# Gated linear attention and a squared-ReLU network on one core: another order of the opening, and attention stretches, weight parts and splits at other places between the products

## The chip, the cores and the metric

The kernel runs on one core of a Trainium2 chip. The core has TensorE (products, PE in the profile, with its weight loads as PEld), VectorE (DVE), ScalarE (ACT), GpSimd (POOL) and SyncE (SP, which issues all transfers here). The metric is the time of one execution on the device, in microseconds; less is better. The profile comes from one execution of its own.

## The reference

Per batch and head, a 48 x 48 state decays by alpha and takes in the outer product of k and v; y is q times the state. The rows of y (all heads side by side, 384 wide) are the input of a network with a squared ReLU.

```python
# B, H, S, D = 4, 8, 768, 48
for t in range(S):
    state = alpha[:, :, t, :, None] * state + einsum('bhd,bhde->...', k[:, :, t], v[:, :, t])
    y[:, :, t] = einsum('bhd,bhde->bhe', q[:, :, t], state)
...
x = y.transpose(0, 2, 1, 3).reshape(3072, 384)
h = np.maximum(x @ w_in, 0.0)          # w_in 384 x 2048
out = (h * h) @ w_out                  # w_out 2048 x 384
```

The weights come in a wider type than fp32: the kernel takes them apart as pairs of 32-bit words and makes fp32 of them.

## The kernel before, in words

**Chunks and groups.** The 768 steps are cut into six pieces of 128; with four batches that makes 24 chunks n = 0 to 23 (`divmod(n, B)` gives piece and batch). Four chunks are one group of 512 rows for the network, so there are six groups g.

**Attention of a chunk.** `ln` takes the logarithm of alpha on ScalarE, `cs` sums it along the rows with a triangular product on TensorE (L280; later chunks as two fp32r halves, L283 and L284, after `sp`). `eb` and `ei` make the factors exp(sum) and exp(-sum), `mq` and `mk` scale q and k with them on VectorE (L299). `qT`, `kT` (L351) or, for later chunks, `turn` (L567) transpose them on TensorE; `qc`, `kc` copy the transposes out of the accumulators. `sc` (L410) makes the scores, `kv` (L438) the state sums, `am` masks the scores, `us` and `st` carry the state on, `lt` or `bl`/`br` bring the last row of factors (through DRAM, L317 and L327). `y` is made for two chunks at a time in two halves: `ga`/`ya` and `gb`/`yb` (L390). `ev` and `ep` copy y into the input x of the network (L605), head pair by head pair.

**The network of a group.** Group 0 runs in plain fp32 (`ffn_in`, L907). From group 1 on a product row is made of three fp32r passes with parts `b`, `l`, `d` of the weights and `a`, `l`, `d` of the data (`in_passes`, L714, for the first layer, and `of_tile`, L797, for the second); part of the second layer of groups 0 and 1 is still plain (`out_plain`). The parts of the data are made by `split_x`, `split_h` (ScalarE a cast L687, VectorE a difference L637) and `diff_x`, `diff_h` (VectorE, L691); the parts of the weights by `prepare`: `cast_w` (L642), `rest_w` (L637), `scale_w` (L656) and `diff_w` (L637), stored to DRAM (L647) and loaded again group by group (`pump`, L680). The wide weights themselves are loaded by L136 and L140 and converted in three steps, `first` (L163, L167), `middle` (L177, L180) and `second` (L188 to L195).

**The order.** It is written out by hand, engine by engine in the order of the calls. The opening is the list of words in `AT['first']`; a word is a step's name with a chunk (and a head pair for `ep`, a name for `load`); `ha`/`hb` are first-layer products of the first or second half of group 0's rows, `warm` and `zeros` are products of zeros that are read by nobody (`zeros` is three fp32 products of 256 columns, six passes). `AT['pre']` is the order of the first loads, `AT['cp']` names the copies of transposes that VectorE does, and `AT['evd']` the evictions of y that VectorE does instead of ScalarE, as (chunk, half, head pair).

After the opening `weave` goes through the list of product rows (`units`) and counts their cost; one unit of cost is called a row here. Everything else is an event with a due time in rows, and is emitted before the first unit that begins at or after it:

```python
def weave(units, events, at):
    for cost, f, args in units:
        while events and events[0][0] <= at:
            _, e, given = events.pop(0)
            e(*given)
        f(*args)
        at += cost
```

The due times are in `AT`: `g0`, `g1`, `g` are the attention stretches woven into group 0, group 1 and later groups (start, first chunk, and for some the place of transposes or of the joined `ga` and `gb`), `sc0` their scale in group 0, `ga` and `gb` the places within a stretch, `evs` and `evs0` the distance of evictions, `w_first`, `w_in_at`, `w_in_by`, `o0`, `o2` the places of `prepare` for weight parts, `str1` the place from which one set of parts is loaded in group 1, `g0x` and `gx` the places of `splits_of_x`, `h0`, `h1` the unit before which splits of h begin, `cv0` the beginning of the weights' conversion.

Of the kernel before, what the change touches and what calls it, by code (L numbers as in the profile page):

```python
# [15 lines left out]


GB = 4
AT = {'evs': 0.65, 'lead': 4, 'post': 3, 'w_first': (45.25, 42.0, 51.5), 'wstep': 1.6, 'w_in_at': 2.5, 'w_in_by': 3.4, 'room1': 22, 'room': 25, 's0': 4, 'ahead': 6, 'late': 2, 'xs': 0.2, 'g0': ((1.5, 4, False, True, 28.25), (20.25, 6, True, True), (28.75, 8, True, False)), 'sc0': (2.35, 2.35, 2.35), 'g1': ((5.5, 8, False, 15.5), (15.5, 10, True), (34.5, 12, True)), 'g': ((1.7, 6, True), (15.5, 8, True)), 'g1x': 50.0, 'gx': 48.25, 'g0x': 55.25, 'k0': 2, 'h0': 16, 'k1': 4, 'h1': 3, 'h1by': 2, 'evs0': 0.3, 'tp': 'ADMD', 'tp1': 'ADAD', 'split': 8, 'o0': (44.75, 47.25), 'o1': (), 'o2': (21.75, 27.5, 31.75, 35.0, 41.25, 41.75), 'str1': 22.0, 'ga': 9.5, 'gb': 13.0, 'cv0': 1.5, 'pre': '0a 1a 0q 0k 1q 1k', 'cp': ('q0', 'k0'), 'evd': ((0, 0, 0), (0, 1, 2), (0, 1, 3), (2, 1, 0), (2, 1, 2)), 'first': 'warm0 load0v ln0 cs0 ln1 zeros3 ei0 eb0 mk0 mq0 kT0 qT0 kc0 cs1 qc0 sc0 eb1 mq1 load2a ei1 ln2 mk1 qT1 kv0 kT1 qc1 weights0 am0 load1v us0 kc1 load2q load3a lt1 sc1 kv1 first0 load2k load3v am1 middle0 cs2 eb2 us1 ei2 ya0 yb0 mk2 ln3 mq2 ep00 ep01 ep02 load2v lt0 qT2 qc2 load3k cs3 kT2 weights2 ep03 kc2 zeros2 sc2 second0 eb3 load3q kv2 first1 ei3 load4v middle1 weights1 mq3 ha0 mk3 qT3 qc3 kT3 kc3 am2 ha1 lt2 second1 sc3 lt3 kv3 st0 load4a us2 load4k am3 us3 ha2 first2 ya2 yb2 load4q ep20 ep21 weights5 ep22 ep23 middle2 st3 ha3 weights3 hb0 hb3 hb2 weights6 weights4 st1 hb1 st2 second2'}


RUN = {0: 128, 32: 32, 64: 64, 96: 32}
# [3 lines left out]
def kernel(  # L26
# [84 lines left out]
    def load(n, xs="aqkv"):  # L111
        c, b = divmod(n, B)
        for x in xs:
            t = tile_of(x, n)
            if id(t) in owner:
                need(("free", *owner[id(t)]))
            owner[id(t)] = x, n
            given.add((x, n))
            nc.sync.dma_start(  # L119
                out=t[:, :, 0:D] if x in "qk" else t.rearrange("a (h d) -> a h d", h=H),  # L120
                in_=srcs[x][b, :, c * C : (c + 1) * C, :].rearrange("h s d -> s h d"),
            )
# [73 lines left out]

    for word in AT["pre"].split():
        load(int(word[0]), word[1:])
# [53 lines left out]
    def work(name, bufs=1):  # L252
        return p2.tile([128, NP, C], FP32, tag=name, name=name, bufs=bufs)
# [7 lines left out]

    SPLIT = AT["split"]

# [98 lines left out]
    def copied(x, n):  # L362
        t = blk[n][f"{x}s"] = work(f"{x}s", 2 if x == "k" else 4)
        copy = nc.vector.tensor_copy if f"{x}{n}" in AT["cp"] else nc.scalar.copy
        copy(out=t, in_=blk[n].pop(f"{x}T"))
# [219 lines left out]
    def ev(n, ps=tuple(range(NP))):  # L585
# [12 lines left out]
        for p in ps:  # L598
            for e, f, end in ((1, 2 * p * D + 32, 2 * (p + 1) * D), (0, 2 * p * D, (2 * p + 1) * D)):
                copy = nc.vector.tensor_copy if (n, e, p) in AT["evd"] else nc.scalar.copy  # L600
                r = 64 * (e ^ p % 2)
# [57 lines left out]
    def diff_w(w, p):  # L659
# [5 lines left out]
        for x in "ld":  # L665
            t = made.pop((x, w, p))
            if w == "i" or p >= NW - AT["k0"] or (x == "l" and p >= NW - AT["k1"]):
                here[x, w, p] = t
        pump()

    def prepare(at, w, p):
        step = AT["wstep"]
        fs = (cast_w, rest_w, scale_w, diff_w)
        return [(at + i * step, f, (w, p)) for i, f in enumerate(fs)]
# [481 lines left out]
```

## Time and profile before

| | us |
|---|---|
| median of 3 runs | 524.77 |
| the 3 runs | 524.69, 524.77, 526.36 |
| the profiled execution | 526.27 |
| its span | 524.5 |
| TensorE busy | 511.0 |
| VectorE busy | 362.1 |
| ScalarE busy | 315.6 |

The granted clock of TensorE is full in every slice. In the table of slices TensorE shows 7 to 9 tenths in the first slices and 9 in nearly all others:

```profile
PE   8799999999999999999999998999999999999997
PEclk9999999999999999999999999999999999999999
```

Each digit is the busy share of a fortieth of the span, 13.1 us; the second line is the granted clock. A busy TensorE counts its products from their modelled beginning to their modelled end, so products that overlap in its pipeline count once. What can be read from the profile is chiefly where TensorE stands still, and which engine, queue or transfer it stands for.

### The profile page before, as it was taken

The page shows a single profiled execution, that of the slowest core. Times are in us where ns is not written, and L with a number is a line of the kernel's source. Part 1 is how long each engine was busy: PE and PEld are TensorE (multiplying, and loading weights), DVE is VectorE, ACT ScalarE, POOL GpSimd, SP SyncE. Part 2 cuts the span into 40 slices and gives each one's busy share as a digit, 9 for nine tenths or more (in the row PEclk, how much of TensorE's full clock was granted, in tenths as well). Part 3 has the DMA queues.
Part 4 walks back from the last instruction along what each step waited for, and adds up shares of the span by engine and source line. Part 5 has one row for each costly group of instructions (what it writes and reads, how often), then busy time and mean ns, then how long its engine had stood idle before and what let it go on. Part 6 is the DMA issues. An engine that isn't in the chain of part 4 may idle for free.

```text
span 524.5 us, 13017 instructions
## 1 busy us (share of the span) xinstructions
PE 511.0 (97%) x5340; PEld 420.8 (80%) x5340; DVE 362.1 (69%) x627; ACT 315.6 (60%) x666; POOL 5.3 (1%) x29
## 2 busy tenths in 40 slices
PE   8799999999999999999999998999999999999997
PEld 6665446558888669988899987799987899988997
DVE  4688979888979679767587455696464485363861
ACT  4769893678799566576954175952265773164620
POOL 4000000000000000000000000000000000000000
PEclk9999999999999999999999999999999999999999
DMA  9999689236598566999886797864684444699201
GB/s 184 201 279 216 196 211 209 47 78 242 180 241 214 153 213 157 310 320 224 199 216 200 248 242 177 221 185 144 214 272 132 158 148 138 224 362 310 82 1 60
DMA packets 139323, 102.35 MB, mean 195 GB/s; under 512 B 109808, under 2 KB 112896, under 8 KB 139264
## 3 DMA queue, kind: packets, MB, share of 16 engines
q1 hardware_dynamic: 139264, 101.52, 68.8%
q8 instruction: 42, 0.69, 0.6%
q14 instruction: 17, 0.14, 0.1%
HBM read 84.17 MB, written 17.33 MB: 194 GB/s over the span
## 4 chain that ended last, share of the span: by engine, by line
PE 87%; SPq 5%; DVE 3%; ACT 2%; DMA 2%; issue 1%; DVEq 0%; ACTq 0%; POOLq 0%
PE o L797 38%; PE h L714 30%; PE h L907 7%; PE y L390 4%; SPq L119 3%; PE T L567 2%; PE sckv L410 2%; PE sckv L438 2%; ACT x L605 1%; DMA qk_lent<-in_q_dram 1%; SPq L327 1%; DVE wl L637 1%; SPq L136 1%; PE cs L283 1%; PE cs L284 1%
## 5 line engine op out<-in xcount | busy, mean ns | idle before, releaser
L714 PE MATMUL h<-xa,wb 128*128 128x512 f32 x240 | 68.8, 395 | 0.6 <-issue 0.5
L714 PE MATMUL h<-xl,wl 128*128 128x512 f32 x240 | 67.8, 391 | 0.0
L714 PE MATMUL h<-xd,wd 128*128 128x512 f32 x240 | 66.6, 392 | 0.0
L731 ACT ACTIVATE h<-h 128x512 f32<-128x512 f32 x40 | 23.3, 581 | 61.7 <-PE h L714 61.5
L605 ACT COPY x<-y 48x256 f32<-48x256 f32 (+3 forms) x136 | 48.5, 364 | 19.1 <-PE y L390 14.9
L637 DVE TENSOR_TENSOR hid<-h,hid 128x512 f32<-128x512 f32 x40 | 27.5, 688 | 44.0 <-PE h L714 41.2
L797 PE MATMUL o<-wd,hd 128*128 128x384 f32 x304 | 53.9, 335 | 0.7 <-DVE osb L834 0.7
L797 PE MATMUL o<-wb,ha 128*128 128x384 f32 x160 | 54.2, 339 | 0.4 <-issue 0.4
L797 PEld LDWEIGHTS o<-wd,hd 128*128 128x128 f32 x304 | 52.7, 188 | 1.2 <-DVE osb L834 1.1
L797 PE MATMUL o<-wl,hl 128*128 128x384 f32 x160 | 53.5, 335 | 0.0
L797 PE MATMUL o<-w_out,hid 128*128 128x384 f32 x160 | 53.5, 490 | 0.0
L714 PEld LDWEIGHTS h<-xl,wl 128*128 128x128 f32 x240 | 45.0, 188 | 10.0 <-DVE xl L637 0.3
L714 PEld LDWEIGHTS h<-xa,wb 128*128 128x128 f32 x240 | 44.3, 188 | 9.9 <-ACT hid L755 0.7
L714 PEld LDWEIGHTS h<-xd,wd 128*128 128x128 f32 x240 | 44.6, 188 | 9.1
L797 PE MATMUL o<-wb,hx 128*128 128x384 f32 x144 | 48.7, 338 | 0.0
L797 PE MATMUL o<-wl,hx 128*128 128x384 f32 x144 | 48.1, 334 | 0.0
L797 PEld LDWEIGHTS o<-w_out,hid 128*128 128x128 f32 x160 | 29.9, 190 | 19.7
L907 PE MATMUL h<-x,w_in 128*128 128x512 f32 (+1 forms) x120 | 43.8, 513 | 0.8 <-ACT x L605 0.7
L687 ACT ACTIVATE ha<-hid 128x512 fp32r<-128x512 f32 x40 | 25.4, 636 | 23.9 <-DVE hx L637 14.4
L729 ACT ACTIVATE hid<-h 128x512 f32<-128x512 f32 x40 | 24.3, 607 | 25.2 <-PE h L714 25.2
L907 PEld LDWEIGHTS h<-x,w_in 128*128 128x128 f32 x120 | 22.1, 190 | 18.8 <-issue 14.8
L637 DVE TENSOR_TENSOR hl<-hid,ha 128x512 fp32r<-128x512 f32 x40 | 27.4, 686 | 12.5 <-ACT ha L687 12.5
(117 smaller groups left out, 879.3 us busy)
## 6 DMA issues: line engine op xcount, KB each, us to landing
wd<-do SPq DMA_DIRECT2D x36, 384.0 KB, 3.1
wl<-lo SPq DMA_DIRECT2D x34, 384.0 KB, 5.0
wl<-li SPq DMA_DIRECT2D x32, 384.0 KB
wd<-di SPq DMA_DIRECT2D x32, 384.0 KB, 4.5
raw<-in_moe_w_in_dram SPq DMA_DIRECT2D x8, 768.0 KB, 6.6
raw<-in_moe_w_out_dram SPq DMA_DIRECT2D x8, 768.0 KB, 4.8
v_in<-in_v_dram SPq DMA_DIRECT2D x24, 192.0 KB, 5.7
out_dram<-osb SPq DMA_DIRECT2D x24, 192.0 KB, 3.1
```

Source lines behind the costliest of these rows:

```text
L119: nc.sync.dma_start(out=t[:, :, 0:D] if x in "qk" else t.rearrange("a (h d) -> a h d", h=H), in_=srcs[x][b, :, c * C : (c + 1) * C, :].rea ...
L390: ins = nc.tensor.matmul(out=ys[e][64 * half : 64 * half + D + G * e, m % 2, p // 2, t], lhsT=lhsT, rhs=rhs, start=(half, e) not in seen, ...
L410: nc.tensor.matmul(out=ps[e][HALF[h], 0, p, :], lhsT=ks[rows, p, HALF[h]], rhs=qs[rows, p, HALF[h]], start=True, stop=True, skip_group_che ...
L438: nc.tensor.matmul(out=ps[h][64 * e : 64 * (e + 1), 1, p, G:64], lhsT=tile_of("k", n)[HALF[h], 2 * p + e, :], rhs=tiles["v"][n % NV][HALF[ ...
L605: copy(out=x[kk][to : to + m, t : t + 2], in_=blk[n]["y"][e][r : r + m, :, p // 2],)
L637: nc.vector.tensor_tensor(out=o, in0=x, in1=z, op=op)
L687: nc.scalar.activation(out=a, in_=x, func=AF.Copy, scale=NEAR)
L714: nc.tensor.matmul(out=acc["h", j], lhsT=here[w, "i", p][:, kk, jj * 128 : (jj + 1) * 128], rhs=x_parts[x][:, kk], start=start and kk == 0 ...
L729: nc.scalar.activation(out=hid[j], in_=x, func=AF.Copy, scale=E)
L731: nc.scalar.activation(out=x, in_=x, func=AF.Copy, scale=1.0 + E)
L797: nc.tensor.matmul(out=acc[t][:, 0:DM], lhsT=lhs[:, t * C : (t + 1) * C], rhs=rhs, start=start, stop=stop, skip_group_check=True,)
L907: nc.tensor.matmul(out=ps, lhsT=w[:, kk, c0 : c0 + 128], rhs=xT[g][kk][:, cols], start=(kk == 0), stop=(kk == KM - 1),)
```

## The change

Only the table `AT` differs; no function does. `...` stands for entries that are the same.

```diff
-'evs': 0.65, 'w_first': (45.25, 42.0, 51.5), 'w_in_at': 2.5, 'w_in_by': 3.4,
+'evs': 0.9, 'w_first': (44.75, 40.75, 52.5), 'w_in_at': 2.375, 'w_in_by': 3.2,
...
-'g0': ((1.5, 4, False, True, 28.25), (20.25, 6, True, True), (28.75, 8, True, False)), 'sc0': (2.35, 2.35, 2.35),
+'g0': ((1.75, 4, False, True, 25.5), (22.25, 6, True, True), (28.25, 8, True, False)), 'sc0': (2.15, 2.35, 2.35),
-'g1': ((5.5, 8, False, 15.5), (15.5, 10, True), (34.5, 12, True)), 'g': ((1.7, 6, True), (15.5, 8, True)),
+'g1': ((5.75, 8, False, 16.25), (15.25, 10, True), (34.5, 12, True)), 'g': ((1.575, 6, True), (15.5, 8, True)),
-'gx': 48.25, 'h0': 16, 'h1': 3, 'evs0': 0.3, 'o0': (44.75, 47.25), 'o2': (21.75, 27.5, 31.75, 35.0, 41.25, 41.75),
+'gx': 46.75, 'h0': 17, 'h1': -1, 'evs0': 0.1, 'o0': (46.75, 47.25), 'o2': (19.5, 28.25, 32.75, 34.0, 42.0, 41.25),
-'str1': 22.0, 'ga': 9.5, 'gb': 13.0, 'cv0': 1.5, 'pre': '0a 1a 0q 0k 1q 1k', 'cp': ('q0', 'k0'),
+'str1': 24.5, 'ga': 9.75, 'gb': 12.75, 'cv0': 1.125, 'pre': '0a 1a 0q 0k 1k 1q', 'cp': (),
-'evd': ((0, 0, 0), (0, 1, 2), (0, 1, 3), (2, 1, 0), (2, 1, 2)),
+'evd': ((0, 0, 0), (0, 1, 0), (0, 1, 2), (2, 0, 2), (2, 1, 1), (2, 1, 2), (2, 1, 3)),
```

The opening's list, cut to the places where it differs most:

```diff
 before
-kT0 qT0 kc0 cs1 qc0 sc0
-load2q load3a lt1 sc1 kv1 first0 load2k load3v
-ya0 yb0 mk2 ln3 mq2 ep00 ep01 ep02 load2v lt0 qT2 qc2 load3k cs3 kT2 weights2 ep03 kc2 zeros2 sc2 second0 eb3 load3q kv2 first1
-ei3 load4v middle1 weights1 mq3 ha0
-ha2 first2 ya2 yb2 load4q ep20 ep21 weights5 ep22 ep23 middle2 st3 ha3 weights3 hb0 hb3 hb2 weights6 weights4 st1 hb1 st2 second2
 after
+kT0 eb0 mq0 cs1 qT0 kc0
+load3a kc1 load2k lt1 sc1 kv1 first0 load2q load2v
+ya0 yb0 mk2 load3v ln3 mq2 qT2 qc2 cs3 ep00 ep01 load3k ep02 kT2 weights1 kc2 zeros2 load3q second0 eb3 lt0 sc2 kv2
+ei3 ep03 zeros3 first1 middle1 weights2 ha0
+ha2 us3 first2 ya2 load4q yb2 weights3 ep20 ep21 ha3 weights4 ep22 ep23 middle2 st3 hb1 second2 weights5 weights6 st2 st1 hb2 hb3 hb0 load4v
```

In the program that comes of it, TensorE has three more fp32 products (the added `zeros3`) and six more semaphore instructions; all other products are the same in number. From group 2 on its order is the same as before. VectorE loses the two copies of transposes of chunk 0 to ScalarE and takes other evictions of chunks 0 to 3. SyncE issues the same transfers; in the opening k stands before q for chunk 1, alpha and k before q for chunk 2 (with chunk 3's alpha first), and the v of chunk 4 behind four more parts of the weights.

More of the change, by code (lines that the diff above doesn't have):

```diff
@@ L18 @@
 GB = 4
-AT = {'evs': 0.65, 'lead': 4, 'post': 3, 'w_first': (45.25, 42.0, 51.5), 'wstep': 1.6, 'w_in_at': 2.5, 'w_in_by': 3.4, 'room1': 22, 'room': 25, 's0': 4, 'ahead': 6, 'late': 2, 'xs': 0.2, 'g0': ((1.5, 4, False, True, 28.25), (20.25, 6, True, True), (28.75, 8, True, False)), 'sc0': (2.35, 2.35, 2.35), 'g1': ((5.5, 8, False, 15.5), (15.5, 10, True), (34.5, 12, True)), 'g': ((1.7, 6, True), (15.5, 8, True)), 'g1x': 50.0, 'gx': 48.25, 'g0x': 55.25, 'k0': 2, 'h0': 16, 'k1': 4, 'h1': 3, 'h1by': 2, 'evs0': 0.3, 'tp': 'ADMD', 'tp1': 'ADAD', 'split': 8, 'o0': (44.75, 47.25), 'o1': (), 'o2': (21.75, 27.5, 31.75, 35.0, 41.25, 41.75), 'str1': 22.0, 'ga': 9.5, 'gb': 13.0, 'cv0': 1.5, 'pre': '0a 1a 0q 0k 1q 1k', 'cp': ('q0', 'k0'), 'evd': ((0, 0, 0), (0, 1, 2), (0, 1, 3), (2, 1, 0), (2, 1, 2)), 'first': 'warm0 load0v ln0 cs0 ln1 zeros3 ei0 eb0 mk0 mq0 kT0 qT0 kc0 cs1 qc0 sc0 eb1 mq1 load2a ei1 ln2 mk1 qT1 kv0 kT1 qc1 weights0 am0 load1v us0 kc1 load2q load3a lt1 sc1 kv1 first0 load2k load3v am1 middle0 cs2 eb2 us1 ei2 ya0 yb0 mk2 ln3 mq2 ep00 ep01 ep02 load2v lt0 qT2 qc2 load3k cs3 kT2 weights2 ep03 kc2 zeros2 sc2 second0 eb3 load3q kv2 first1 ei3 load4v middle1 weights1 mq3 ha0 mk3 qT3 qc3 kT3 kc3 am2 ha1 lt2 second1 sc3 lt3 kv3 st0 load4a us2 load4k am3 us3 ha2 first2 ya2 yb2 load4q ep20 ep21 weights5 ep22 ep23 middle2 st3 ha3 weights3 hb0 hb3 hb2 weights6 weights4 st1 hb1 st2 second2'}
@@ new lines @@
+AT = {'evs': 0.9, 'lead': 4, 'post': 3, 'w_first': (44.75, 40.75, 52.5), 'wstep': 1.6, 'w_in_at': 2.375, 'w_in_by': 3.2, 'room1': 22, 'room': 25, 's0': 4, 'ahead': 6, 'late': 2, 'xs': 0.2, 'g0': ((1.75, 4, False, True, 25.5), (22.25, 6, True, True), (28.25, 8, True, False)), 'sc0': (2.15, 2.35, 2.35), 'g1': ((5.75, 8, False, 16.25), (15.25, 10, True), (34.5, 12, True)), 'g': ((1.575, 6, True), (15.5, 8, True)), 'g1x': 50.0, 'gx': 46.75, 'g0x': 55.25, 'k0': 2, 'h0': 17, 'k1': 4, 'h1': -1, 'h1by': 2, 'evs0': 0.1, 'tp': 'ADMD', 'tp1': 'ADAD', 'split': 8, 'o0': (46.75, 47.25), 'o1': (), 'o2': (19.5, 28.25, 32.75, 34.0, 42.0, 41.25), 'str1': 24.5, 'ga': 9.75, 'gb': 12.75, 'cv0': 1.125, 'pre': '0a 1a 0q 0k 1k 1q', 'cp': (), 'evd': ((0, 0, 0), (0, 1, 0), (0, 1, 2), (2, 0, 2), (2, 1, 1), (2, 1, 2), (2, 1, 3)), 'first': 'ln0 warm0 ln1 cs0 zeros3 ei0 mk0 kT0 eb0 mq0 cs1 qT0 kc0 eb1 load0v load2a qc0 mq1 sc0 ei1 ln2 qT1 mk1 kv0 weights0 qc1 am0 load1v us0 kT1 load3a kc1 load2k lt1 sc1 kv1 first0 load2q load2v am1 middle0 cs2 eb2 us1 ei2 ya0 yb0 mk2 load3v ln3 mq2 qT2 qc2 cs3 ep00 ep01 load3k ep02 kT2 weights1 kc2 zeros2 load3q second0 eb3 lt0 sc2 kv2 ei3 ep03 zeros3 first1 middle1 weights2 ha0 mq3 mk3 qT3 load4k qc3 kT3 kc3 am2 load4a ha1 second1 sc3 lt2 lt3 kv3 st0 am3 us2 ha2 us3 first2 ya2 load4q yb2 weights3 ep20 ep21 ha3 weights4 ep22 ep23 middle2 st3 hb1 second2 weights5 weights6 st2 st1 hb2 hb3 hb0 load4v'}
```

## The prediction

> **What bounds the kernel now.** I read the page's head first, then TensorE's waits after the opening, the order in time around them, the fetch queue, and last the opening.
>
> ```profile
> span 524.5 us, 13017 instructions
> ...
> PE 511.0 (97%) x5340; PEld 420.8 (80%) x5340; DVE 362.1 (69%) x627; ACT 315.6 (60%) x666; POOL 5.3 (1%) x29
> ```
>
> TensorE is busy for 97%. Only its idle time, 13.2 us when I add its gaps, can be won: about 3.5 us behind its last product, 1.1 us before its first, 4.4 us in the opening up to 38.5 us, and this after 40 us:
>
> ```profile
> PE y L390 <- issue: 2.5, 2, 1.6
> PE o L797 <- DVE osb L834: 0.7, 1, 0.7
> PE h L714 <- issue: 0.5, 1, 0.5
> PE o L797 <- issue: 0.4, 1, 0.4
> ```
>
> "Issue" means that nothing in the profile was waited for. In the order in time two of these cut a run of `y` products (L390) in the middle; 318.52 is the larger.
>
> ```profile
> 316.40 0.22 PE L390 MATMUL y<-am,v_in 64*48 64x64 f32 x1
> 316.41 0.24 PE L390 MATMUL y<-qs,us 48*64 48x64 f32 x2
> 316.44 0.48 PE L390 MATMUL y<-am,v_in 64*48 64x64 f32 x18
> 318.52 0.45 PE L390 MATMUL y<-am,v_in 64*64 64x64 f32 x13 [1.59 <-issue]
> ```
>
> I numbered TensorE's instructions in the program's order: a plain fp32 product is two weight loads and two products, a transpose or an fp32r product one of each, and semaphore instructions count. The four interrupted ones are numbers 2241, 7361, 8129 and 9153, at 103.19, 316.92, 346.04 and 398.79 us, for 0.92, 1.59, 0.41 and 0.54 us. Their distances are 20, 3 and 4 times 256. The queue list says what comes in such portions:
>
> ```profile
> q8 instruction: 42, 0.69, 0.6%
> ```
>
> 0.69 MB in 42 packets is 16.4 KB each, and 10,816 instructions are 42.25 times 256. So TensorE's program comes in blocks of 256, and block k+1 (beginning at 256k+193) is fetched about when block k begins. The four waits end 1.33 to 1.60 us after their packet has landed (packets 0.94 to 2.06 us). From a block's beginning to the next being usable were, in the blocks that start inside dense work, about 2.8 to 6 us, mostly 3.4 to 4.5. A dense stretch (scores L410, sums L438, `y` L390) runs 278 instructions in some 2.15 us, so a block lying wholly in one runs dry. Beside rows of L714 (227 ns a product) or L797 (173 or 323 ns) a block lasts over 8 us.
>
> One wait is of another kind; TensorE stands at 126.16 until VectorE has read the output sums:
>
> ```profile
> 126.90 3.04 PE L797 MATMUL o<-wd,hd 128*128 128x384 f32 x16 [0.74 <-DVE osb L834]
> ```
>
> The opening ends with waits for the last evictions of `y`, after which TensorE runs unbroken:
>
> ```profile
> 36.65 1.48 PE L907 MATMUL h<-x,w_in 128*128 128x256 f32 x4 [0.34 <-ACT x L605]
> 38.47 5.87 PE L907 MATMUL h<-x,w_in 128*128 128x256 f32 x23 [0.34 <-ACT x L605]
> ```
>
> **The change part by part.**
>
> *Numbering.* From the third output group on, TensorE's order stays the same, but everything has a number 18 higher: six more `zeros` passes (12 instructions) and six semaphore instructions. Block edges so lie 9 products (18 instructions) earlier against the work. What decides is how far before a block's beginning its trigger comes. In even flow packets start when TensorE executes 11 to 40 instructions ahead of the block's first one, since its sequencer runs ahead; in the packet before 74.50 us that was 4.5 us. If the edge lies under about 20 instructions inside a dense stretch, that lead reaches back into the slow products before it.
>
> - Edge 1985 (wait at 103): it was 26 products into the stretch and is 11; before it stand L797 products of 323 ns. Packet 8 started 0.97 us after the stretch began; five products of lead are 1.6 us. The next block is needed 0.25 us earlier. 0.92 becomes 0 to 0.9; I take -0.9.
> - Edge 7105 (wait at 317): 20 becomes 11, before it L714. About 1.2 us earlier, and before the `wd` loads that shared its 2.06 us. 1.59 becomes 0 to 1.6; I take -1.4.
> - Edge 8897 (wait at 399): 17 becomes 8. I take -0.5, between -0.54 and 0.
> - Edge 7873 (wait at 346) gets worse: 30 becomes 21, still inside, and the slow L797 products at the block's end drop by 9, so that it ends 9 x 173 ns = 1.56 us sooner. Its packet came 2.67 us after the block's beginning, at a DMA share of 0.99, where packet 8 had found 0.06 (stretch, its length, TensorE's busy time and instructions, granted clock, DMA share, GB/s):
>
> ```profile
> 101.70:102.70 1.00, 1.00 (x83) 1.00 0.06 16
> ...
> 344.00:345.00 1.00, 1.00 (x7) 1.00 0.99 288
> ```
>
>   If the packet comes as late, +1.56; if 1.4 us sooner, +0.2. I take +1.1.
> - Edge 5313: the block would last about 5.05 us instead of 6.15 and its successor took 5.1. +0.1 (0 to 0.7).
> - Edge 1473: the scores of chunks 4 and 5 now come earlier, so this edge stands one product before four runs of 32. L907 products of 430 ns lie before it; the lead covers it. 0 (to 0.9).
>
> *The wait at 126.* The last split and casts were queued on VectorE until 126.29. Now only 16 plain L797 products follow `gb` and four stand behind the next `ga`; four more rows of L797 x 2 (8 x 323 ns = 2.6 us) were done before. From the end of `gb` I add ScalarE's queue (12 evictions at 0.385, 3 splits at 0.53, 2 casts and 3 scalings at 0.75, 4 outputs at 0.38): the last split ends at 10.8 us, VectorE's L834 can start at 14.1, TensorE comes at 15.0. So 0.74 may vanish; a ScalarE late by a us gives it back, by two 0.9 more. I take -0.6.
>
> *Opening.* Up to 15.6 us the second `v` load decides (a wait of 1.36), at 26.1 us the load of the fourth `q`; both keep their place in SyncE's queue, with the same bytes ahead. Alpha and `k` now go before the third `q`, which saves 0.5 us at 20.3, but not behind 26.1. The six added `zeros` passes (6 x 217 ns = 1.3 us) fill the time until VectorE's conversion (24.8) and the last eviction (about 25.5); uncovered they cost 0.4. The two copies that leave VectorE (0.69 each) cost ScalarE 0.57 each before 10.4, under the wait for `v`. Evictions of the second pair go 5 to VectorE (0.44) and 8 pieces to 7 on ScalarE, done near 38.2 instead of 38.4. Against that, edge 1217 is now inside the products before that, and packet 4 was usable at about 36.95: a wait of up to 1 us, half of it hidden by the evictions. The conversion of weight part 3 is due at 42.2 against a use at 42.68 either way. +0.3 (-0.5 to +1.0).
>
> *Rest.* The `v` load moved behind four weight parts is issued near 41 instead of 21 us and lands in 6, with its use past 70. In group 1 the split of `hid` 8 stands before the last plain row: 0.53 + 0.61 us under a row of 1.3 and transposes of 1.15. Weight casts, weight loads and splits of `x` move by up to 2.5 rows; VectorE's writes of weight parts in group 1 end 1.0 us and more before TensorE's use. Three late evictions per group step behind a split, while ScalarE is free. Nothing; should one queue slip, its nearest margins (0.1 to 0.4 us at 275 to 285) are the price.
>
> **Sum.** -0.9 - 1.4 - 0.5 + 1.1 + 0.1 - 0.6 + 0.3 = -1.9 us. The profiled execution took 526.27 us (span 524.5), 1.5 above the median of 524.77 and beside the slowest of the three, so 524.4 by its account. Which wait the faster runs lacked no trace tells; I carry the -1.9 to the median unchanged: 522.9 us.
>
> [...]
>
> **Rivals.**
> - *The lead does not reach* (slower). Packets start no earlier than the dense stretch, because its first products wait or the fetch queues behind other transfers. For it: packets 4 and 31 came 3.69 and 2.67 us after their block began. Against: packets in slow rows started up to 4.5 us ahead. It decides as soon as packets 8, 28 and 35 start after the first L410 product: the three waits stay, edge 7873 costs its full 1.56, and edge 1217 in the opening 0.8: 527.1.
> - *VectorE and ScalarE keep the gain.* TensorE reaches L834 2.6 us closer to `gb`, and ScalarE's queue slips by two: +0.9 in place of -0.6, or the same at 275 us: 524.4 to 525.5.
> - *All waits go.* Packet 31 comes early as well (its 0.41 vanishes): -3.46 - 0.74 and the opening even: 520.6.
> - *The waits are not fetches*, and shifting edges does nothing: -0.6 + 0.3: 524.5. The 256 speaks against it. [...]
>
> **How the numbers follow.** 0.3% of 524.77 is 1.6 us, about what a measurement of this kernel can tell; faster means below 523.2, slower above 526.3. Forecast 0.45 (0.37 of it below 523.2), lead does not reach 0.21 (0.20 above 526.3), engines keep the gain 0.15 (0.12 within), all waits go 0.14, not fetches 0.05 (0.04 within). Faster 0.51, same 0.25, slower 0.24. The forecast's own range is 521.6 to 524.4; with the outer cases 520.8 to 527.2 holds eight in ten.
>
> **What would show it.** Issue waits at 103, 317 and 399 gone, and one of 1 to 2 us at number 8129 inside the `o` products of L797; no wait for L834; TensorE unbroken from 38.2 to 38.9 us. A packet landing later than 1.3 us before its edge without a wait, or issue waits away from 193 modulo 256, would prove the fetch account wrong. A new wait on ScalarE or VectorE in group 1 would make the time wrong.

## The result and the profile after

| | before | after |
|---|---|---|
| median of 20 runs each, us | 525.8 | 527.25 |
| lowest and highest | 524.25 to 528.62 | 525.48 to 529.12 |
| ratio of times | 1 | 1.0028 (95% interval 1.0017 to 1.0040) |
| profiled execution, us | 526.27 | 526.31 |
| its span | 524.5 | 524.5 |

The change costs 1.5 us (0.9 to 2.1). The forecast was 522.9, a gain of 1.9, with a range that ended at 527.2. The two profiled executions are equally long; the difference stands in the medians alone. I come back to that, because it is part of what went wrong.

The head of the page of after, then TensorE's waits behind 40 us (engine, line, what was waited for, us in total, times, longest):

```profile
span 524.5 us, 13040 instructions
...
PE 511.1 (97%) x5346; PEld 422.1 (80%) x5346; DVE 363.2 (69%) x627; ACT 317.1 (60%) x666; POOL 5.3 (1%) x29
```

```profile
PE o L797 <- issue: 1.7, 1, 1.7
PE y L390 <- issue: 0.9, 2, 0.6
PE h L907 <- ACT x L605: 0.8, 1, 0.8
PE h L714 <- issue: 0.4, 1, 0.4
```

Against the list of before: the wait for L834 is gone, one of the two large waits of `y` is gone and the other is smaller, `o` waits for nothing visible for 1.7 instead of 0.4 us, and the opening's end waits 0.8 us for an eviction. In the order in time (start, length, tile and shape, number of products, and in brackets the idle time before them):

```profile
126.42 2.93 PE L797 MATMUL o<-wd,hd 128*128 128x384 f32 x16
...
316.24 0.35 PE L390 MATMUL y<-am,v_in 64*48 64x64 f32 x9
317.23 0.57 PE L390 MATMUL y<-am,v_in 64*64 64x64 f32 x22 [0.65 <-issue]
...
342.94 0.33 PE L797 MATMUL o<-wb,ha 128*128 128x384 f32 x1
344.98 0.34 PE L797 MATMUL o<-wl,hl 128*128 128x384 f32 x1 [1.71 <-issue]
```

The first line had 0.74 us of idle time before it and has none. `y` is cut after 9 products of its last kind, where it was after 18: the block edge has moved by nine products, as 18 instructions would move it. The last line is instruction 8129. All waits for "issue" over 0.2 us still stand at numbers that leave 193 when divided by 256, or (the one at 399) at the product whose weight load has such a number. The opening's end is new:

```profile
34.51 1.35 PE L907 MATMUL h<-x,w_in 128*128 128x256 f32 x5
37.93 1.24 PE L907 MATMUL h<-x,w_in 128*128 128x256 f32 x5 [2.07 <-issue]
40.01 6.30 PE L907 MATMUL h<-x,w_in 128*128 128x256 f32 x24 [0.84 <-ACT x L605]
```

After five of the first half products of step `ha3` TensorE stands for 2.07 us, at number 1217, and 2 us later it stands again for ScalarE. ScalarE's own order tells why there are two waits:

```profile
34.64 1.91 ACT L605 COPY x<-y 32x256 f32<-32x256 f32 x5 [1.10 <-PE y L390]
38.34 0.38 ACT L913 ACTIVATE r<-h 128x256 f32<-128x256 f32 x1 [1.79 <-PE h L907]
38.76 0.42 ACT L916 ACTIVATE hid<-r 128x256 f32<-128x256 f32 x1
39.20 0.75 ACT L605 COPY x<-y 32x256 f32<-32x256 f32 x2
```

In the kernel before all eight of ScalarE's evictions ran in one piece:

```profile
35.33 3.09 ACT L605 COPY x<-y 48x256 f32<-48x256 f32 x8 [1.56 <-DVE x L605]
```

In the new order `ha3` stands between the evictions of `y`. Its sixth product comes only after the edge, ScalarE waits 1.79 us for it (L913), and the two evictions behind it in the queue (39.20) are late by as much. So the edge holds up the very evictions that were to hide it. The first product of 512 columns, with which the half products are over, begins in the trace at 44.43 instead of 42.89: 1.54 us later. I call that moment the end of the half products from here on.

### The profile page after: what moved, and what is told of

The parts are those of the page before. It is cut to its first block, busy times and chain, and to the rows that moved or that the text cites. A ratio compares the mean times of both kernels' runs of the same rounds, so it can differ in the third digit from the quotient of the medians.

```text
span 524.5 us, 13040 instructions
## 1 busy us (share of the span) xinstructions
PE 511.1 (97%) x5346; PEld 422.1 (80%) x5346; DVE 363.2 (69%) x627; ACT 317.1 (60%) x666; POOL 5.3 (1%) x29
## 4 chain that ended last, share of the span: by engine, by line
PE 92%; SPq 3%; DMA 1%; issue 1%; ACT 1%; DVE 0%; POOLq 0%; DVEq 0%
PE o L797 41%; PE h L714 32%; PE h L907 7%; PE y L390 4%; SPq L119 3%; PE T L567 2%; PE sckv L410 2%; PE sckv L438 2%; DMA raw<-in_moe_w_in_dram 1%; PE cs L283 1%; PE cs L284 1%; PE cs L280 0%; SPq L136 0%; ACT power L177 0%; ACT hid L916 0%
## 5 line engine op out<-in xcount | busy, mean ns | idle before, releaser
L605 ACT COPY x<-y 32x256 f32<-32x256 f32 (+3 forms) x134 | 48.3, 364 | 18.7 <-PE y L390 16.4
L637 DVE TENSOR_TENSOR hid<-h,hid 128x512 f32<-128x512 f32 x40 | 27.5, 688 | 44.7 <-PE h L714 41.9
L637 DVE TENSOR_TENSOR hl<-hid,ha 128x512 fp32r<-128x512 f32 x40 | 27.5, 686 | 11.6 <-ACT ha L687 11.5
```

Of the source, the lines that this page charges most:

```text
L605: copy(out=x[kk][to : to + m, t : t + 2], in_=blk[n]["y"][e][r : r + m, :, p // 2],)
L637: nc.vector.tensor_tensor(out=o, in0=x, in1=z, op=op)
```

## The experiments

Times are medians of their own comparison, and ratios are to the kernel before, run on the same chip beside them.

### Both kernels once more

No edit. One execution of each was traced so far; these are the second ones.

> The kernel before, unchanged, once more. All theories: 525.8 us and a ratio of 1.000 within 0.002. What it is for: its second profiled execution shows whether the waits at the 256-instruction edges (0.92 us at 103, 1.59 at 317, 0.41 at 346, 0.54 at 399 in the first) keep their sizes from one execution to the next. Theory A (a wait is set by the transfer of the next block, whose length depends on the other transfers under way at that moment): the places stay, each size within 0.5 us of the first. Rival: the places move too, and then the waits are no fetches.

> The kernel after, unchanged, once more. All theories: 527.25 us within 0.8. What it is for: a second profiled execution. Theory A: the wait at edge 1217 (2.07 us before) is there again at the same instruction, between 0.2 and 2.6 by how late the transfer of block 4 starts, and the late waits stand at the same instructions with other sizes (0 to 2 each). Rival: one or more of these places is free of a wait in this execution and others take their place; then the waits are not bound to the edges.

Before again: 526.26 us, ratio 1.000 (0.998 to 1.002). After again: 527.42, 1.0022 (0.9997 to 1.0046). Here are the waits of TensorE for the block at 36 (those for evictions beside it, 0.3 to 0.8 us, are left out) and all its waits over 0.2 us from 45 us on, by their place in the program (the last two columns belong to an experiment below). The places at 36, 103, 240, 317, 344 and 399 are block edges. The 1.11 in the last column the profile puts down to VectorE (L637); it stands at the edge, 1.41 us after its packet landed.

| about | before | again | after | again | three small ahead | behind |
|---|---|---|---|---|---|---|
| 36, number 1217 | 0 | 0 | 2.07 | 0.92 | 1.96 | 0 |
| 103, number 2241 | 0.92 | 0.92 | 0 | 0 | 0 | 0 |
| 126, L834 | 0.74 | 0.73 | 0 | 0 | 0 | 0 |
| 213 and 221, parts of the weights | 0 | 0.23 | 0 | 0.88 | 0.74 | 0.43 |
| 240 (before again: VectorE, L637) | 0 | 0.92 | 0.43 | 0.43 | 0.72 | 0.45 |
| 317, number 7361 | 1.59 | 1.03 | 0.65 | 1.70 | 0.37 | 0.90 |
| 344, number 8129 | 0.41 | 0 | 1.71 | 0.74 | 1.67 | 1.11 |
| 399, number 9153 | 0.54 | 0 | 0.26 | 0 | 0 | 0.24 |
| sum behind 45 | 4.20 | 3.83 | 3.05 | 3.76 | 3.50 | 3.13 |

The places stay with the numbering, the sizes do not, and they scatter by more than the half microsecond that I expected: 317 had 0.65 in one execution of the kernel after and 1.70 in the other. Only the waits at 103 and 126 before and the one at 240 after repeat to 0.01 us. A second finding is in the windows of after again (stretch, its length, busy time and instructions of PE, PEld, DVE, ACT and POOL, granted clock, DMA share, GB/s):

```profile
316.00:318.00 2.00, 0.81 (x57) 0.69 (x47) 1.97 (x6) 0.92 (x2) 0.00 (x0) 1.00 1.04 307
318.00:320.00 2.00, 1.49 (x26) 1.24 (x26) 1.60 (x5) 0.00 (x0) 0.00 (x0) 0.90 0.76 219
320.00:322.00 2.00, 2.00 (x6) 1.61 (x5) 0.00 (x0) 0.52 (x1) 0.00 (x0) 0.50 0.01 3
322.00:324.00 2.00, 2.00 (x8) 1.53 (x8) 0.00 (x0) 0.07 (x1) 0.00 (x0) 0.74 0.00 0
```

Behind the wait of 1.70 us the granted clock goes to 0.50 and is back by 324. By the column, as an estimate, that is 0.10 x 2 + 0.50 x 2 + 0.26 x 2 = 1.7 us of lost clock: in this execution the wait and the lost clock behind it come to twice the wait's length.

### The openings exchanged

```diff
 in AT, the entries 'pre', 'cp', 'evd' and 'first' alone
-(those of before)                     +(those of after)     before_open_of_after
-(those of after)                      +(those of before)    after_open_of_before
```

> The kernel before with the new opening alone (the list of steps, the preload, the copies and the evictions of it); the late moves are left as they were. Theory A (the loss is the opening's: the edge at instruction 1217 now falls inside the first half product and its block comes late): the wait of about 2 us at 36 is there as in the kernel after, the late edges shift by about 13 instructions, so that the wait at 346 grows to about 1.7 and those at 103, 317 and 399 shrink by 0.3 to 0.9 each; time 526.0 to 527.5, in the profile the end of the half products 1.2 to 1.8 us later than before. Rival B (the late moves of stretches and splits cost the time, the opening does not): no change, 525.5 to 526.1.

> The kernel after with the old opening; the late moves stay. Theory A (the opening's edge 1217 costs): the end of the half products comes back by about 1.5 us, edge 1217 lies at the end of the first half product again and its wait is under 0.6; late waits as in the kernel after; time 525.3 to 526.2, about 1.4 us below the kernel after. Rival B (the late moves cost the time): 527 to 527.5, as the kernel after.

The late moves with the old opening: 524.52 us, ratio 0.9966 (0.9939 to 0.9992), so a gain of 1.8 (0.4 to 3.2), more than expected (525.3 to 526.2). Its half products end at 42.59, and neither 103 nor 126 has a wait. The old late places with the new opening: 527.48, ratio 1.0014 (0.9990 to 1.0038); that comparison decides nothing alone, and its profile is a miss: 0.24 us at edge 1217 and the half products at 42.72, where a wait of about 2 and 1.2 to 1.8 us of delay were expected. Packet 4 had come 2.89 us after its block began, against 4.89 in the kernel after. So the opening costs the time in the one pair, but by a wait whose size changes; what in it costs was still to be shown.

### Without the added zero products

```diff
-... kv2 ei3 ep03 zeros3 first1 ...
+... kv2 ei3 ep03 first1 ...
```

> The kernel after without the added zero products of block 3 (12 TensorE instructions ahead of the first half product); its list of steps is otherwise the new one. Theory A (the opening lost because the edge at instruction 1217 fell after five of the first half products, not after ten or eleven, so that its block was waited for): the edge is back behind the eleventh of them, its wait is under 0.4 us, the end of the half products comes 1.3 to 2.5 us earlier than the 44.43 of the kernel after, late waits as in the run with the old opening (0.6 to 1.0 each at 316, 343 and 397); time 524.0 to 525.5. Rival B (the new order of loads and evictions in the opening costs the time by itself): the half products end within 0.8 us of 44.4, time 526.5 to 527.5.

524.99 us, ratio 0.9969 (0.9950 to 0.9988): taking these 12 instructions, and one semaphore instruction with them, out of 10,834 makes the kernel after faster than the kernel before. The half products end at 42.80. The late waits are not the expected ones: 1.64 at 315, 0.19 at 344 and none at 397, where three of 0.6 to 1.0 were expected. But both the numbering has changed and a row of zero products is gone, 1.56 us long in the kernel after (from 23.66).

### Three small products, ahead or behind

The zero products of block 3 keep their number and lose their columns; they stand at their place, ahead of the first half-product step, or behind the fifth (`hb1`), 15 half products later (the second expectation says six). (The zero products at the beginning are called with 1 instead of 3 here and stay large.)

```diff
+out=ps[:, 0:NP, :] if n != 3 else ps[0:D, 0, 0:1], lhsT=...[:, 0 : 128 if n != 3 else D],
+rhs=s_t[3] if n != 3 else s_t[3][:, 0, 0:1], ...
...
 ahead:   ... ep03 zeros3 first1 ... ha3 ... st3 hb1 second2
 behind:  ... ep03 first1 ... ha3 ... st3 hb1 zeros3 second2
```

> The kernel after with the three added zero products of block 3 cut from 256 columns to one, at their place ahead of the first half product: the numbering is that of the kernel after to the instruction, their work (2.5 us of products in rows of 0.41 each) nearly gone. Theory A (the edge at 1217 costs, by its place): the wait at it stays or grows, since the block's transfer does not start sooner; the half products end at 43.0 to 44.6; time 526.2 to 527.5. Rival D (the work of the zero products was the loss): the half products end 1.6 us sooner than with them, as in the run without them, time 524.8 to 525.5.

> As the run with three small products ahead, but the three stand behind the half products of the second set (six products later) instead of ahead of the first: the same instructions, the same numbering from there on; only edge 1217 moves, from behind the fifth half product to behind the eleventh. Theory A: no wait over 0.4 at edge 1217, the half products end at 42.4 to 43.3, 0.6 to 2 us sooner than with the three ahead; late edges as in the kernel after, so that its late waits (0.4 at 240, 0.6 to 1.7 at 317, 0.7 to 1.7 at 343 to 346) stay; time 525.0 to 526.2. Rival D: the same time as with the three ahead, within 0.4.

Ahead: 527.47 us, ratio 1.0031 (1.0004 to 1.0059). Behind: 525.76, ratio 0.9996 (0.9978 to 1.0015). The order in time of the first, then of the second:

```profile
34.47 1.35 PE L907 MATMUL h<-x,w_in 128*128 128x256 f32 x5
37.77 1.24 PE L907 MATMUL h<-x,w_in 128*128 128x256 f32 x5 [1.96 <-issue]
```

```profile
34.37 2.40 PE L907 MATMUL h<-x,w_in 128*128 128x256 f32 x8
37.12 0.70 PE L907 MATMUL h<-x,w_in 128*128 128x256 f32 x2 [0.35 <-DVE x L605]
38.10 0.70 PE L907 MATMUL h<-x,w_in 128*128 128x256 f32 x2 [0.28 <-ACT x L605]
38.73 0.43 PE L378 MATMUL zeros<-s 128*48 128x1 f32 x6
```

The two kernels hold the same instructions, but for one semaphore instruction. Where 12 of them stand ahead, the edge cuts the products after the fifth; where they stand behind, TensorE goes through it, and the half products end at 43.08 instead of 44.27. Leaving nearly all of the zero products' work out changes little (44.43 to 44.27). Packet 4 started alike in both, 4.59 and 4.24 us after its block. So it is the edge's place, and neither the work nor the order of loads that the two share. (The intervals of the two ratios touch; that the edge costs is told by the traces, how much in the median only roughly.)

What decides is how much work lies between the beginning of block 4 and edge 1217: 5.2 us in the kernel after, 7.5 to 7.8 where the edge comes after ten or eleven products. Packet 4 came 2.9 to 4.9 us after that beginning in the seven traces with the new opening whose edge 1217 lies in the half products; add its 0.9 to 1.1 us and 1.5 until TensorE goes on, and 5.2 is too short in each of them and 7.5 enough. The one later start, 5.12 us in the run with the old opening, needed 7.6.

### All edges moved, by small products

```diff
 def zeros(n):
-    for _ in range(3):
+    for _ in range(2 if begins else 3):
 ...
+    for _ in range(29 if begins else 0): nc.tensor.matmul(out=ps[0:D, 0, 0:1], lhsT=...[:, 0:D],
+        rhs=s_t[3][:, 0, 0:1], start=True, stop=True, skip_group_check=True)
```

> The kernel after with one of the three zero products ahead of the first block replaced by 29 products of one column, which moves every block edge behind them 112 instructions earlier in the work and changes nothing else. Theory A (the waits behind 200 us are waits for blocks): the waits of 0.43 at 240, 0.65 at 317, 1.71 at 343 and 0.26 at 399 (3.05 together) go, since each dense stretch of small products then lies inside a block with at least 4.8 us of other products behind its beginning; the opening's edge 1217 falls into the y products ahead of its second half product and still waits 1 to 3 us; the small products cost 0 to 1 us in the wait for the first loads; time 523.5 to 525.5. Rival C (these waits are the attention's own, for banks or operands that the profile does not show): the waits stay at the same lines with the same sizes, 527 to 528.

529.13 us, ratio 1.0036 (1.0015 to 1.0056): the time was a miss, the waits were not. Its list behind 40 us:

```profile
PE o L797 <- DMA wd<-do: 0.8, 1, 0.8
PE h L907 <- DVE x L605: 0.3, 1, 0.3
PE h L907 <- ACT x L605: 0.3, 1, 0.3
PE h L714 <- issue: 0.2, 1, 0.2
```

Of 3.05 us of fetch waits 0.15 is left, and the edge in the opening still waits (2.52 us, now in `y`). From the end of the half products on this kernel gains 2.7 us on the kernel after. Up to there it had lost 4.2 (48.66 against 44.43), and the windows show where:

```profile
8.00:10.00 2.00, 2.00 (x48) 2.00 (x47) 0.17 (x1) 0.00 (x0) 0.00 (x0) 1.00 1.47 190
10.00:12.00 2.00, 2.00 (x14) 1.37 (x13) 0.00 (x0) 0.58 (x1) 0.00 (x0) 0.67 1.08 288
12.00:14.00 2.00, 1.32 (x12) 0.83 (x13) 0.56 (x1) 1.30 (x3) 0.00 (x0) 0.50 1.18 291
14.00:16.00 2.00, 2.00 (x40) 1.55 (x42) 0.56 (x1) 0.58 (x2) 0.00 (x0) 0.50 1.07 168
16.00:18.00 2.00, 2.00 (x46) 1.74 (x46) 0.86 (x3) 0.69 (x2) 0.00 (x0) 0.63 1.28 195
```

TensorE counts as busy in all of 8 to 10 us with the small products, and yet the granted clock falls to 0.50 right behind them, for about 6.8 us (an estimate from the column, with a clock of 1.00 or 0.50: 1.32 + 4 + 1.48). Of this kernel's 11 runs only one has a mean granted clock of 0.999 or more, so this execution is probably not the only one.

### The late edges moved alone

To move the late edges without touching the opening, products of 512 columns in the first layer of group 0 (behind edge 1217) are cut into two of 256: the same columns, four instructions more for each.

```diff
+ps, m = ..., n // 2 if g == 0 and n == GB * C and len(halved) < 9 and not halved.append(j) else n
-for kk in range(KM):
+for kk, e in [(kk, e) for e in range(0, n, m) for kk in range(KM)]:
+    nc.tensor.matmul(out=ps[:, e : e + m], ..., rhs=xT[g][kk][:, cols.start + e : cols.start + e + m], ...)
```

With 9, 5 or 10 in place of the 9; the last kernel has it without the zero products and with the new opening.

> The kernel after with the old opening, and with the first nine full-width half-sets of the first layer (27 products of 512 columns) each cut into two products of 256 columns: the same columns, 108 TensorE instructions more, which moves every edge from 1473 on by 108 instructions and leaves edge 1217 alone. Theory A: the late waits of the run with the old opening (0.77 at 316, 0.82 at 343, 0.95 at 397, 2.54 together) go to under 0.5 together; the cuts cost 0 to 1.5 us, since a weight load of 190 ns lies under the product before it; time 522.0 to 524.0, 0.5 to 2.5 below the run with the old opening (524.5). Rival C (these waits are the attention's own): they stay, and the time is 524.5 to 526.

> As the run with nine cut sets, but with five (15 products, 60 instructions): less added work than nine, and the worse numbering by the account of fetches. Theory A: a wait of 2 to 3.5 us at about 236, where the edge now falls behind a short block of attention products, and one of 0.8 to 2 at about 261; those at 316 and 397 go; time 525.5 to 527.0, 2.5 to 4.5 above the run with nine. Rival C (only the added work counts): between the run with no cuts (524.5) and the one with nine, no new waits.

> The kernel after with the old opening and ten sets cut into halves: 30 products more, numbering 13 instructions beyond the run with nine, as it was in the run with the 28 small products, which had no late wait over 0.15. Theory A: the waits of 0.71 at 234 and 0.94 at 260 of the run with nine go, no wait at an edge over 0.3 behind 45 us; time 522.5 to 524.3, below the run with nine (525.0) by 0.5 to 2. Rival C (the cuts cost, not the edges): as the run with nine or slower.

> The kernel after without the added zero products, with ten sets cut into halves: the new opening with the numbering of the run with the 28 small products, less 8. Theory A: the late waits of the run without the zero products (1.64 at 315, 0.19 at 344) go, edge 1217 stays free; time 522.5 to 524.3, 0.7 to 2.5 below that run (525.0), and the fastest of the study beside old_open_split10. Rival C: 525 or slower.

| cuts | median | ratio | waits at edges behind 45 us, one execution each |
|---|---|---|---|
| none, old opening | 524.52 | 0.9966 (0.9939 to 0.9992) | 0.77, 0.82, 0.96 |
| 5 | 529.79 | 1.0061 (1.0031 to 1.0090) | 3.45, 2.62 |
| 9 | 525.04 | 0.9962 (0.9940 to 0.9983) | 0.71, 0.94 |
| 10 | 522.34 | 0.9926 (0.9902 to 0.9951) | none |
| 10, new opening without zeros3 | 522.54 | 0.9937 (0.9913 to 0.9960) | none |

Five cuts add the least work and are slowest by far; ten add the most and are fastest. So the cuts cost little, and the numbering decides. With five, the edges fall at 238 and 269 behind short blocks:

```profile
237.90 0.54 PE L390 MATMUL y<-am,v_in 64*48 64x64 f32 x19
241.89 0.69 PE L390 MATMUL y<-am,v_in 64*48 64x64 f32 x12 [3.45 <-issue]
```

The expectation of 525.5 to 527.0 for it was too low: in the profiled execution the waits were longer, and the granted clock fell to 0.50 at both. (That execution took 536.07 us, more than the median, and its clock was at 0.50 in the opening too, from about 15.3 to 25.5 us by the windows; its waits tell the places, not the usual sizes.) Nine cuts were a miss: I had placed their edges too far from the dense stretches, 0.71 and 0.94 us came up at 234 and 260, and the median did not fall. Part of that is the clock: among runs with a mean granted clock of 0.999 or more the median is 523.19 with nine cuts (5 of 12 runs) against 523.96 with none (9 of 12), and with five cuts no run of the 12 reaches 0.999. Thirteen instructions more, with ten cuts, and the list of TensorE's waits behind 40 us has one line:

```profile
PE o L797 <- DMA wd<-do: 1.4, 1, 1.4
```

This kernel beats both: 522.34 us, 3.9 us (2.6 to 5.2) below the kernel before. With the waits gone the two openings come out alike (522.34 and 522.54).

## Why the prediction was wrong, step by step

In the prediction's list an edge is the number at which a block begins; the wait is for the block behind it and stands 256 numbers further on. Only "edge 1217" names the place of the wait itself.

**The fetch account held.** In all 14 traces every issue wait over 0.2 us stands at a block's edge (193 modulo 256, or the product behind it), moves with the numbering, and goes when the numbering lets it. No block's first instruction comes sooner than 0.87 us after its packet has landed, and none without a wait sooner than 1.41, so the sign that the prediction named against itself (a packet later than 1.3 us without a wait) did not come. The rival that the waits are no fetches is out. That TensorE's sequencer runs ahead of its products stands in the trace of before too: ahead of the block that begins at 74.50 us, the semaphore instruction of L280 is recorded at 71.7, the weight load of that line at 73.4, and the packet starts at 70.0.

**The step that failed is the opening's**, "+0.3 (-0.5 to +1.0)", and in it "packet 4 was usable at about 36.95: a wait of up to 1 us, half of it hidden by the evictions". Measured: usable at 37.93, 36.77 and 37.77 in three executions, waits of 2.07, 0.92 and 1.96, and nothing hidden, since two of the evictions stand behind `ha3` in ScalarE's queue. The end of the half products is at 43.85 on the mean of the two executions of after against 42.51 for before: +1.3. The size depends on when the packet starts: in the four traces with the edge behind the fifth product of that stretch the end lies at 42.72 to 44.43, in five with the edge five or six products further on at 42.13 to 43.08. Everything else of that step was right: with the edge out of the way the new opening ends at 42.80 and 43.08, which is the +0.3 or little more, and the work of the zero products is hidden.

**The second step that failed is edge 7105**, "1.59 becomes 0 to 1.6; I take -1.4". The mean of two executions goes from 1.31 to 1.18, by -0.1. The lead that I counted on was not there: packet 28 started 0.45 us after its block in the kernel after.

**One execution was taken for the kernel.** The base was off: 524.77 was the median of 3 runs, that of 20 is 525.8. Edge 8897 (-0.5) had 0.54 in one execution of before and nothing in the next; edge 5313 (+0.1) measured 0.43 in both of after; the loads of weight parts at 213 and 221, which I did not have, add 0.3 on the mean. The waits behind 45 us add up to 4.02 on the mean of two for before and 3.40 for after: a gain of 0.6, where the terms, without the opening, add up to 2.2. With +1.3 from the opening that makes +0.7, without the 1.7 us of clock that one of the two executions of after lost. Among the runs whose mean granted clock was 0.999 or more the median is 525.82 for before (57 runs) and 526.84 for after (19 runs), +1.0. The comparison's 1.5 has 0.9 as its lower end, so a few tenths stay open: two traced executions of each are too few for them.

**What was right.** Edge 1985 (-0.9): gone in all traces of the new numbering, 0.92 in both of before. The wait for L834 (-0.6): 0.74 gone, and still 0.99 where the late places were left as they were. Edge 7873 (+1.1): 0.41 and 0 became 1.71 and 0.74. Edge 1473: 0. The late moves under the old opening gain 1.8 us.

**The rivals.** "The lead does not reach" named 527.1 and comes nearest, by two of its prices, edge 1217 and the full 1.56 at edge 7873 (1.30 more in the first pair). Its main claim, that the waits at 103, 317 and 399 stay, is wrong for 103: packet 8 started 1.50 us before its block. Its sum also leaves out the -0.6 for L834, which came; with it the sum would be 526.5, so that 527.1 lies so near 527.25 in part by luck. That VectorE and ScalarE would keep the gain at L834 did not happen.

## What to carry to other kernels

Where TensorE's program is long and has stretches of tiny products, look for waits for "issue" at equal distances in instructions (here multiples of 256); then a few instructions more or less anywhere ahead can be worth microseconds (here thirteen more, from nine cuts to ten, came with 2.7 us less), and splitting a large product is a cheap way to move all edges behind it (here 30 split products stand in each of the two fastest kernels). Before an edge is moved off one place, look where every other edge lands, the opening's among them, and what stands behind the held-up product in the other engines' queues. Take the size of such a wait from several executions (0.65 and 1.70 us at 317 in the kernel after), and look in the windows behind each wait whether the granted clock fell as well: its length alone did not tell here (0.50 behind one of 1.70 us, 1.00 through one of 2.07).

## What the hardware showed beyond that

- The granted clock of TensorE fell to 0.50 after a wait of 1.70 us among tiny products (317, after again) and in the opening with five cuts (0.82 in the stretch from 14 to 16 us, in which TensorE stands for 1.40 us, and 0.50 in the next), and in another execution it stayed at 1.00 through waits of 2.07 (36, after) and 1.71 (344, after). A run of one-column products came before a fall with TensorE busy throughout (from 8 us on, 28 small products): being busy by the profile did not hold the clock there. By the windows, an estimate that takes the clock as 1.00 or 0.50, the stretches at 0.50 lasted 3.4 us (317, after again: 0.4 + 2 + 1.04) and 6.8 us (behind the small products, and at 238 with five cuts: 1.44 + 4 + 1.40). What makes the clock fall no run here shows.
- The same opening had its fourth packet of instructions 0.61 us (ten cuts) and 5.12 us (old opening) after the block began. From 32 to 36 us the DMA share is 1.02 and 1.04 in these two traces and 1.01 in the kernel after, with the weights and the first chunks on their way; the packet's own transfer takes 0.9 to 1.3 us in all of them, so it is the start that is late. What sets the start no run here shows.
